# Root chains per group, placed behind GpSimd's output transfers, with the sums of y held back for VectorE's half sums

## The chip, the cores and the metric

The kernel runs on one core of one Trainium2 chip. The metric is the device time of one execution in microseconds (us). One profiled execution of the kernel before is at hand, and seven timed ones.

## The reference, cut to what matters

The input x has 8 sequences of 4224 rows with 192 channels. The first stage is a causal convolution along the rows with 7 taps, whose weights are a softmax per head (8 heads of 24 channels). Its result is called y here. The second stage normalises each row and adds a small network of two matrix products to it:

```python
w = softmax(weight)                                   # 8 heads x 7 taps
y = conv(x_padded, w)                                 # per head, 7 rows back
xn = (y - mean(y)) / sqrt(var(y) + 1e-6) * g_ln
out = y + maximum(xn @ w_ch1, 0) @ w_ch2              # 192 -> 768 -> 192
```

The kernel folds the mean and g_ln into w_ch1. The factor 1/sqrt(var + 1e-6) is positive, so it can be taken out of the relu and applied to the rows of the result at the very end. It is therefore not needed until a row's two products are done.

## The kernel before

**Groups.** The rows are cut into 18 groups (`groups`). Groups 0 to 2 are small (6, 8 and 10 columns of 128 rows). Groups 3 to 17 have 16 columns each, two groups per sequence. A loop over the groups does, for group g, an *up* stage (192 to 768, `up_mixed`) and a *down* stage (768 to 192, `down_fast`); the convolution of g + 1 and the first taps of g + 2 are woven in between. All instructions stand in the order in which the program writes them; each engine takes its own in that order, and semaphores make an engine wait for another one's results. So what stands ahead of an instruction on its engine holds it up.

**Products.** In groups 3 to 17 both stages are done with seven block products instead of eight, on the quarters of the operands. That needs sums of quarters. In the up stage these are sums of y: s3 and s2 (`sums_of_y`, L575 and L576, on GpSimd, called POOL in the profile), then s4 and the sum written over a21 (L578 and L579, on VectorE, DVE in the profile). TensorE (PE) takes first a11 and a12, which need no sum, then s2, s3, s1 (this is a21 with L579 in it), a22, s4, for one third of the hidden units, and then again in another order for the other two thirds. In the down stage PE does three products, then a fourth one, and meanwhile DVE does nine *half sums* in place (`half_sum`, L756, 128x1024 elements each): three for the fifth product, three for the sixth, three for the seventh. Three additions from PSUM (L820) follow on DVE.

**The row statistics.** `moments` lets DVE write six numbers per row (L439, 16 instructions). `root` makes 1/sqrt(var + 1e-6) of them on GpSimd, with 19 small instructions (L457 to L470) on a tile of one column per column of rows: two reads of the statistics, then a start value, and three Newton steps of four instructions each. Before the change one chain of `root` serves two groups, 3 with 4, 5 with 6, and so on: `chain_of` says which group's tile holds the statistics, and the call stands at the end of the loop's turn for odd g, after `down_fast(g)`, in which the moments of g + 1 are taken. Group 17 has a chain of its own.

**GpSimd's queue.** It also issues DMAs that add into their target. In one turn of the loop its instructions are, in order: three transfers in `up_mixed` that add a part of a product into the hidden tile (L583, room<-room), one more of each of two larger kinds (L583, parts_cs and parts_tb), two output transfers of the group before (L876, `add_to_out`), two transfers that add the second tap into y of g + 2 (L397, `second_tap`), the two sums of y of g + 1 (L575, L576), in odd turns `root`, and at the start of even turns a memset of padding rows (L160). The third of the L583 transfers must have landed before ScalarE (ACT) can overwrite what it read, and PE waits for that.

**ScalarE's list of work.** `up_mixed` returns a list (`work`) of ACT instructions that `down_fast` puts between the evictions of its first products: a relu, the scaling of the rows of the group before (with the two `add_to_out` behind the last of each half), two more relus; `down_fast` adds the first and second taps of g + 2 to it. Nine entries go behind the first product, six behind the second and six behind the third. With 17 entries ahead of the taps, both output transfers are issued by then; the second tap's transfers are the last entry, behind the later products. In the last group the list holds the three relus alone.

Of the kernel before, what the change touches and what calls it, by code (L numbers as in the profile page):

```python
# [16 lines left out]
def kernel(  # L17
# [29 lines left out]
    nc = tc.nc  # L47
# [377 lines left out]
    def chain_of(g):  # L425


        return g - g % 2 if g < 3 else g - 1 + g % 2

    def moments(g, j1=0, j2=None):  # L430
        n = groups[g][2]
        if j1:
            pass
        elif g == chain_of(g):
            sums[g] = spool.tile([P, 2 * J, nc.vector.BN_STATS_DIM], F32, tag="st", name=f"st{g}")
        else:
            sums[g] = sums[g - 1][:, groups[g - 1][2] :]
        for j in range(j1, n if j2 is None else j2):
            nc.vector.bn_stats(out=sums[g][:, j, :], in_=y[g][:, j, :])  # L439

    def root(g):
        both = [k for k in (g, g + 1) if k < NG and chain_of(k) == g]
        n = sum(groups[k][2] for k in both)
        st = sums[g]
        dt = spool.tile([P, 2 * J], F32, tag="d", name=f"d{g}")
        vt = spool.tile([P, 2 * J], F32, tag="v", name=f"v{g}")
        rt = spool.tile([P, 2 * J], F32, tag="r", name=f"r{g}")
        d, v, r = dt[:, 0:n], vt[:, 0:n], rt[:, 0:n]

        def affine(dst, src, scale, bias):  # L450
            nc.gpsimd.tensor_scalar(
                out=dst, in0=src, scalar1=scale, scalar2=bias, op0=ALU.mult, op1=ALU.add
            )

        nc.gpsimd.tensor_tensor(d, st[:, 0:n, 1], st[:, 0:n, 4], op=ALU.subtract)  # L457
        nc.gpsimd.tensor_tensor(v, st[:, 0:n, 2], st[:, 0:n, 5], op=ALU.add)
        nc.gpsimd.tensor_tensor(d, d, d, op=ALU.mult)
        affine(v, v, 1.0 / D, 1e-6)  # L460
        affine(d, d, 0.25, 0.0)
        nc.gpsimd.tensor_tensor(v, v, d, op=ALU.add)


        affine(r.bitcast(I32), v.bitcast(I32), -0.5, float(0x5F3759DF))
        for _ in range(3):
            nc.gpsimd.tensor_tensor(d, r, r, op=ALU.mult)  # L467
            nc.gpsimd.tensor_tensor(d, d, v, op=ALU.mult)
            affine(d, d, -0.5, 1.5)
            nc.gpsimd.tensor_tensor(r, r, d, op=ALU.mult)  # L470
        for k in both:
            rstd[k] = rt[:, (k - g) * groups[g][2] :]
# [95 lines left out]
    def sums_of_y(g, engine):  # L568

        room = upool.tile([P, 3 * HJ * CH * C], F32, tag="ys", name=f"ysums{g}")  # L570
        room = room.rearrange("p (v j c t) -> p v j c t", v=3, c=CH, t=width(g))
        s2, s3, s4 = [room[:, v] for v in range(3)]
        a11, a12, a21, a22 = quarters_of_y(g)
        ysums[g] = a21, s2, s3, s4
        engine.tensor_tensor(s3, a21, a11, op=ALU.subtract)  # L575
        engine.tensor_tensor(s2, s3, a22, op=ALU.add)  # L576
        yield
        nc.vector.tensor_tensor(s4, a12, s2, op=ALU.subtract)  # L578
        nc.vector.tensor_tensor(a21, a21, a22, op=ALU.add)  # L579
        yield  # L580
# [4 lines left out]
    def up_mixed(g, ahead):  # L585
# [103 lines left out]
        p.close(p.c22, Y, rooms[1][:, 0:PAIR])  # L689
        p.product(X, a22, p.t[2], False)  # L690
        p.relu(p.c11)
        lower_sum(g, (PAIR,))
        p.close(p.c21, X)
        p.product(Y, s4, p.b22, False)
# [7 lines left out]
        taps_of_next(5, 6, heads=(H // 2, H))  # L702
        taps_of_next(6, K)

        work = [lambda: one.relu(one.c22)]

        def scale_one(j):
            scale(g - 1, j, j + 1)
            if j == 7:
# [1 line left out]
            elif j == done - 1:  # L711
                add_to_out(g - 1, 8, done)

        if not last:
            work += [lambda j=j: scale_one(j) for j in range(2, done)]
        half = [lambda i=i: two.relu(two.c22[:, i : i + 1]) for i in range(PAIR)]
        return work[0:9] + half + work[9:]

# [53 lines left out]
    def down_fast(g, work):  # L772
        n = fast[g]
        t = width(g)
        w = n * T
        a = of_products(g)
        flat = cpool.tile([P, NC, NFAST * C], F32, tag="cs", name=f"cs{g}")[:, :, 0 : n * C]
        order = "p c (h j t) -> p c h j t" if t == C else "p c (j h t) -> p c h j t"
        cs = flat.rearrange(order, h=2, t=t)
        free = a[:, 1, 0].rearrange("p f q j t -> p (f q) j t")  # L780
        parts = [free[:, 0:CH], free[:, CH : 2 * CH]]
        banks = [take_bank() for c in range(CH) for i in range(2)]

        def product(bank, left, right, to, first, behind=0):
            for c in range(CH):
                dst = banks[2 * c + bank]
                for f in (PAIR, *range(PAIR)):
                    for q in range(NQ):
                        nc.tensor.matmul(  # L789
                            dst[C * q : C * q + C, 0:w], right[:, f, C * c : C * c + C],  # L790
                            left[:, f, q], start=(first and f == PAIR), stop=(f == PAIR - 1),
                            skip_group_check=True,
                        )
                if to is not None:
                    nc.scalar.copy(  # L795
                        to[:, c], dst[:, 0:w].rearrange("p (j t) -> p j t", t=t)
                    )
                for one in work[:behind]:
                    one()
                del work[:behind]  # L800

        b = quarters_of_w2()
        c11, c21 = cs[:, 0:CH, 0], cs[:, 0:CH, 1]
        c12, c22 = cs[:, CH:NC, 0], cs[:, CH:NC, 1]
        if g + 2 < NG:
            work += [
                lambda tap=tap, h=h: tap(g + 2, heads=(h, h + 1))
                for tap in (first_tap, second_tap) for h in range(H)
            ]
        product(0, a[:, 0, 0], b[0], c11, True, 3)  # L810
        product(1, a[:, 1, 0], w2sums[:, 2], c22, True, 2)
        product(1, a[:, 1, 1], w2sums[:, 3], c21, False, 2)
        product(1, a[:, 0, 1], b[2], None, True, 3)
        if g + 1 < NG:
            transpose(g + 1)
        half_sum(g, (1, 1), (1, 1), (1, 0), ALU.add)
        half_sum(g, (0, 0), (1, 1), (0, 0), ALU.add)
        half_sum(g, (0, 1), (0, 1), (1, 1), ALU.subtract)
        for c in range(CH):
            nc.vector.tensor_tensor(  # L820
                c11[:, c], c11[:, c], banks[2 * c + 1][:, 0:w].rearrange("p (j t) -> p j t", t=t),
                op=ALU.add,
            )
        product(0, a[:, 1, 1], w2sums[:, 1], parts[0], False, 2)
        product(0, a[:, 0, 0], w2sums[:, 0], parts[1], False, 2)
        for one in work:
            one()
        product(0, a[:, 0, 1], b[3], c12, False)
        if g + 1 < NG:
            moments(g + 1)  # L830
            sums = sums_of_y(g + 1, nc.gpsimd)
            next(sums)
            next(sums)
        else:
            finish_fast(g, 0, flat, cs, parts)
        return flat, cs, parts
# [105 lines left out]
    for g in range(NG):  # L942
        mixed, last = g in MIXED, g + 1 == NG
        if g + 2 < NG:
            load_x(g + 2)
        if mixed:
            work = up_mixed(g, ahead(g))
        else:
            up(g)
        if not fast[g]:  # L950

            conv(g + 1)
            transpose(g + 1)
            if g < 2:
                store_y(g + 1)
                moments(g)
            first_tap(g + 2)
            if g == 2:

                second_tap(g + 2)  # L960
                store_y(g + 1, nc.gpsimd)
            down(g)
            park(g)
            if g == 1:
                finish(0)
                root(0)
                sums_of_quarters([w2sums[:, v] for v in range(4)], *quarters_of_w2())
                moments(2)
                root(2)
                finish(1)  # L970
            elif g == 2:
                b11, b12, b21, b22 = quarters_of_w1()
                sums_of_quarters([b12] + [w1sums[:, v] for v in range(3)], b11, b12, b21, b22)
                later = sums_of_y(3, nc.vector)
                next(later)
                next(later)
                finish(2)
                moments(3)
            continue
        if g + 2 < NG:  # L980
            store_y(g + 1)
        results = down_fast(g, work)
        if last:
            finish_fast(g, 1, *results)
            add_and_store(g, slice(0, fast[g]))
            down(g)
            finish(g)
        else:
            if g % 2:
                root(g)  # L990
            if g + 2 == NG:
                root(g + 1)


# [28 lines left out]
```

## Time and profile before

| what | value |
|---|---|
| median of 7 timed runs | 985.5 us (983.26 to 987.48) |
| the profiled execution's own time | 985.5 us |
| its span in the trace | 983.8 us |
| granted TensorE clock, mean | 0.992 |
| TensorE matmul busy | 956.4 us, 97% |
| VectorE busy | 902.5 us, 92% |
| ScalarE busy | 680.8 us, 69% |
| GpSimd busy | 261.9 us, 27% |
| a down stage without a stall | 27.44 us |
| an up stage without a stall | 27.95 to 27.96 us |

The span is 1.7 us shorter than the time of the execution; that lies around it. A busy TensorE is not TensorE at its peak, but in this kernel the same 504 matmuls take the same time in every stage that has no stall, so that a longer stage tells of a wait. The rows of a timeline give the start in us, the time taken, the engine, the line, the operation and the tiles (written <- read); the brackets hold the idle time of the engine before it, and what ended it.

### The profile page before, as it was taken

The page shows a single profiled execution, that of the slowest core. Times are in us where ns is not written, and L with a number is a line of the kernel's source. Part 1 is how long each engine was busy: PE and PEld are TensorE (multiplying, and loading weights), DVE is VectorE, ACT ScalarE, POOL GpSimd, SP SyncE. Part 2 cuts the span into 40 slices and gives each one's busy share as a digit, 9 for nine tenths or more (in the row PEclk, how much of TensorE's full clock was granted, in tenths as well). Part 3 has the DMA queues.
Part 4 walks back from the last instruction along what each step waited for, and adds up shares of the span by engine and source line. Part 5 has one row for each costly group of instructions (what it writes and reads, how often), then busy time and mean ns, then how long its engine had stood idle before and what let it go on. Part 6 is the DMA issues. An engine that isn't in the chain of part 4 may idle for free.

```text
span 983.8 us, 38335 instructions
## 1 busy us (share of the span) xinstructions
PE 956.4 (97%) x17274; PEld 722.5 (73%) x17274; DVE 902.5 (92%) x1491; ACT 680.8 (69%) x1098; POOL 261.9 (27%) x383
## 2 busy tenths in 40 slices
PE   5999999999999999999999999999999999998997
PEld 5886586676968677685968678686867768695787
DVE  5899998979999899989999898989999899999757
ACT  4733769467786968777795868778695867775351
POOL 2004411612116131432117131432217121342200
PEclk8999999999999999999999999999999999999999
DMA  8343687579687796978787796968877796756031
GB/s 171 121 123 131 146 210 180 150 151 252 139 240 155 180 235 116 272 151 243 149 226 157 168 245 122 275 129 239 164 194 174 146 279 136 185 120 109 2 67 67
DMA packets 26386, 165.15 MB, mean 168 GB/s; under 512 B 3567, under 2 KB 4463, under 8 KB 18542
## 3 DMA queue, kind: packets, MB, share of 16 engines
q0 software_dynamic: 19120, 99.36, 51.7%
q1 hardware_dynamic: 6798, 63.34, 17.4%
q8 instruction: 135, 2.21, 0.9%
q14 instruction: 29, 0.24, 0.1%
q10 hardware_dynamic: 304, 0.00, 0.0%
HBM read 38.95 MB, written 50.33 MB: 91 GB/s over the span
## 4 chain that ended last, share of the span: by engine, by line
PE 77%; DVE 8%; DMA 7%; POOL 4%; ACT 2%; issue 1%; SPq 0%; ACTq 0%; DVEq 0%; POOLq 0%
PE ps L521 37%; PE ps L789 34%; PE ps L736 6%; DVE room L756 6%; DMA room<-room 5%; DVE st L439 2%; DMA xg<-in_x_dram 1%; ACT room L616 1%; POOL d L457 1%; PE ps L320 1%; POOL d L467 1%; POOL room L583 1%; DMA ga<-in_moe_g_ln_dram 1%; POOL r L470 1%; DVE room L622 0%
## 5 line engine op out<-in xcount | busy, mean ns | idle before, releaser
L408 DVE SCALAR_TENSOR_TENSOR y<-xg,taps,y 128x384 f32<-128x384 f32 (+3 forms) x734 | 367.2, 578 | 2.4 <-ACT y L383 2.0
L789 PE MATMUL ps<-room,w2sums 128*32 128x256 f32 (+1 forms) x4320 | 237.4, 377 | 4.1 <-DVE room L756 3.1
L521 PE MATMUL ps<-yt,w 32*128 32x256 f32 (+2 forms) x4104 | 238.6, 379 | 0.0
L616 ACT COPY room<-ps 128x1024 f32<-128x1024 f32 (+1 forms) x132 | 172.0, 1303 | 85.8 <-PE ps L521 78.6
L521 PEld LDWEIGHTS ps<-yt,w 32*128 32x128 f32 x4104 | 203.6, 185 | 27.5 <-issue 7.0
L789 PEld LDWEIGHTS ps<-room,w2sums 128*32 128x32 f32 x4320 | 140.5, 110 | 96.2 <-DVE room L756 6.7
L789 PE MATMUL ps<-room,w 128*32 128x256 f32 (+1 forms) x3240 | 180.3, 375 | 2.5 <-DVE room L756 2.4
L756 DVE TENSOR_TENSOR room<-room 128x1024 f32<-128x1024 f32 (+1 forms) x135 | 157.8, 1242 | 7.6 <-PE ps L789 7.6
L789 PEld LDWEIGHTS ps<-room,w 128*32 128x32 f32 x3240 | 105.1, 110 | 70.4 <-DVE room L622 5.2
L521 PE MATMUL ps<-ysums,w1sums 32*128 32x256 f32 x2160 | 124.1, 377 | 0.0
L521 PEld LDWEIGHTS ps<-ysums,w1sums 32*128 32x128 f32 x2160 | 110.7, 185 | 9.6 <-issue 2.7
L795 ACT COPY cs<-ps 128x256 f32<-128x256 f32 (+1 forms) x180 | 66.4, 372 | 45.6 <-PE ps L789 45.6
L629 ACT ACTIVATE room<-room 128x1024 f32<-128x1024 f32 (+1 forms) x75 | 90.8, 1236 | 10.2 <-DMA room<-parts_cs 9.9
L869 ACT ACTIVATE ot<-ot,r 128x192 f32<-128x192 f32 x232 | 93.8, 463 | 0.0
L876 POOL DMA_DIRECT2D out_dram<-ot x40 | 34.4, 1084 | 206.0 <-ACT ot L869 127.8
L622 DVE TENSOR_TENSOR room<-room,ps 128x2048 f32<-128x2048 f32 (+1 forms) x20 | 42.5, 2128 | 47.0 <-PE ps L521 46.8
L383 ACT ACTIVATE y<-xg,taps 128x384 f32<-128x384 f32 (+3 forms) x141 | 72.8, 611 | 9.6 <-DMA out_dram<-y 6.9
L521 PE MATMUL ps<-yt,w1sums 32*128 32x256 f32 x1080 | 66.6, 386 | 5.3 <-ACT room L616 5.3
L439 DVE BATCH_NORM_STATS2 st<-y 128x6 f32<-128x192 f32 x264 | 70.2, 342 | 0.0
L795 ACT COPY room<-ps 128x256 f32<-128x256 f32 (+1 forms) x90 | 33.8, 375 | 48.5 <-PE ps L789 44.5
L521 PE MATMUL ps<-ysums,w 32*128 32x256 f32 x1080 | 64.8, 378 | 0.0
L521 PEld LDWEIGHTS ps<-yt,w1sums 32*128 32x128 f32 x1080 | 54.7, 189 | 12.8 <-ACT room L616 9.8
(103 smaller groups left out, 905.9 us busy)
## 6 DMA issues: line engine op xcount, KB each, us to landing
xg<-in_x_dram SPq DMA_DIRECT2D x15, 2112.0 KB, 17.6
out_dram<-ot POOLq DMA_DIRECT2D x29, 768.0 KB, 8.8
y<-tb POOLq DMA_DIRECT2D x28, 768.0 KB, 10.7
room<-room POOLq DMA_DIRECT2D x42, 512.0 KB, 5.9
out_dram<-y SPq DMA_DIRECT2D x13, 1536.0 KB, 10.1
room<-parts_cs POOLq DMA_DIRECT2D x14, 1024.0 KB, 8.9
room<-parts_tb POOLq DMA_DIRECT2D x14, 1024.0 KB, 7.5
xg<-in_x_dram SPq DMA_DIRECT2D x1, 1536.0 KB, 7.5
```

The lines of the kernel that those rows point to most:

```text
L383: nc.scalar.mul(y[g][:, 0:n, cs], xg[g][:, 0:n, cs], taps[:, h, 0:1])
L408: nc.vector.scalar_tensor_tensor(out=y[g][:, 0:n, cs], in0=t[:, k : k + n, cs], scalar=taps[:, h, k : k + 1], in1=y[g][:, 0:n, cs], op0=AL ...
L439: nc.vector.bn_stats(out=sums[g][:, j, :], in_=y[g][:, j, :])
L521: nc.tensor.matmul(banks[:, q, i * w : i * w + w], right[rows, c, P * i : P * i + P], left[rows, :, c, :], start=(first and c == 0 and i = ...
L616: nc.scalar.activation(dst, src, AF.Relu) if relu else nc.scalar.copy(dst, src)
L622: nc.vector.tensor_tensor(c, c, self.seen(banks), op=ALU.add)
L629: nc.scalar.activation(c, c, AF.Relu)
L736: nc.tensor.matmul(bank[C * q : C * q + C, 0:w], w2[:, f, C * c : C * c + C], left, start=(f == 0), stop=(f == NF - 1),)
L756: nc.vector.tensor_tensor(a[:, *dst, f], a[:, *left, f], a[:, *right, f], op=op)
L789: nc.tensor.matmul(dst[C * q : C * q + C, 0:w], right[:, f, C * c : C * c + C], left[:, f, q], start=(first and f == PAIR), stop=(f == PAI ...
L795: nc.scalar.copy(to[:, c], dst[:, 0:w].rearrange("p (j t) -> p j t", t=t))
L869: nc.scalar.mul(ots[g][:, j, :], ots[g][:, j, :], rstd[g][:, j : j + 1])
```

## The change

There are five edits.

1. `chain_of`: only groups 0 and 1 share a chain; each later group has its own, with tiles of 16 columns instead of 32.
2. `root(g)` is called in `down_fast(g)`, after the third product. On GpSimd it stands behind both output transfers (L876) and ahead of the second tap's transfers (L397) and of the sums of y of g + 1 (L575, L576). The calls at the end of the loop's turn go.
3. In `sums_of_y` on GpSimd, DVE first sets one element of s3 to zero. GpSimd's first sum overwrites it and so waits for DVE to come to that memset, which stands behind the half sums and the three additions.
4. The order in the program becomes: memset, the two GpSimd sums, the moments of g + 1 on DVE, and the two DVE sums. In each engine's own order only the memset is new.
5. In the last group the relus of the two parts of c22 are done in `up_mixed`, ahead of `lower_sum`, the second part as one instruction instead of two; the list of work is empty.

```diff
     def chain_of(g):
-        return g - g % 2 if g < 3 else g - 1 + g % 2
+        return 0 if g < 2 else g
...
-            sums[g] = spool.tile([P, 2 * J, nc.vector.BN_STATS_DIM], F32, tag="st", name=f"st{g}")
+            sums[g] = spool.tile([P, J, nc.vector.BN_STATS_DIM], F32, tag="st", name=f"st{g}")
...
-        dt = spool.tile([P, 2 * J], F32, tag="d", name=f"d{g}")
+        dt = spool.tile([P, J], F32, tag="d", name=f"d{g}")
...
         ysums[g] = a21, s2, s3, s4
+        if engine is not nc.vector:
+            nc.vector.memset(s3[:, 0:1, 0:1, 0:1], 0.0)
         engine.tensor_tensor(s3, a21, a11, op=ALU.subtract)
...
         p.relu(p.c11)
+        if last:
+            one.relu(one.c22)
+            p.relu(p.c22)
         lower_sum(g, (PAIR,))
...
-        work = [lambda: one.relu(one.c22)]
-        if not last:
-            work += [lambda j=j: scale_one(j) for j in range(2, done)]
+        if last:
+            return []
+        work = [lambda: one.relu(one.c22)]
+        work += [lambda j=j: scale_one(j) for j in range(2, done)]
...
         product(1, a[:, 1, 1], w2sums[:, 3], c21, False, 2)
+        root(g)
         product(1, a[:, 0, 1], b[2], None, True, 3)
...
         if g + 1 < NG:
-            moments(g + 1)
             sums = sums_of_y(g + 1, nc.gpsimd)
             next(sums)
+            moments(g + 1)
             next(sums)
...
-        else:
-            if g % 2:
-                root(g)
-            if g + 2 == NG:
-                root(g + 1)
```

## The prediction on record

> **What bounds the kernel now.** The page's first part comes first: TensorE is busy for 956.4 of 983.8 us. I then cut the trace at PE's stage boundaries and looked at those stretches one by one, since 504 equal matmuls take 27.95 us in an up stage and 27.44 us in a down stage when nothing waits. The table by stretches has the stretch, its length, then busy us (and instructions) of PE, PEld, DVE, ACT and POOL, the granted clock and DMA:
>
> ```profile
> 154.94:184.97 30.03, 27.64 (x508) 16.52 (x505) 30.00 (x40) 20.85 (x45) 8.04 (x6) 1.00 0.87 232
> 184.97:216.82 31.85, 29.93 (x508) 26.55 (x504) 26.43 (x44) 20.27 (x17) 13.76 (x25) 0.95 0.55 110
> 411.33:439.29 27.96, 27.96 (x508) 25.36 (x504) 25.63 (x41) 20.02 (x17) 13.52 (x25) 1.00 0.75 151
> 522.38:551.35 28.97, 28.25 (x509) 25.26 (x505) 25.48 (x42) 20.27 (x17) 13.77 (x25) 1.00 0.72 146
> 579.09:607.04 27.95, 27.95 (x507) 25.35 (x504) 25.27 (x40) 19.88 (x17) 4.33 (x5) 1.00 0.74 148
> 887.60:919.90 32.30, 29.20 (x509) 16.06 (x505) 32.11 (x45) 15.17 (x36) 8.09 (x5) 0.95 0.41 71
> ```
>
> The reader should see that most stages are already at their floor, and that the excess sits in few: the down stages of groups 3 (first row) and 16 (last), and up stages of even groups, where POOL has 25 instructions instead of 5. That is the root chain. The chain of waits around up(10) says how it reaches PE:
>
> ```profile
> 522.49 2.66 POOL d L457
> ...
> 533.46 1.16 POOL room L583 x2
> 534.62 9.32 DMA room<-room
> ...
> 544.04 1.88 ACT room L616
> ```
>
> L583 stands behind root on POOL. It is issued about 8 us later than in an odd group, lands at 543.94, and ACT, then PE, wait. The two down stages have another cause, seen in the timeline of group 16:
>
> ```profile
> 899.80 13.51 DVE L756 TENSOR_TENSOR room<-room 128x1024 f32<-128x1024 f32 x9
> 900.03 2.65 POOL L575 TENSOR_TENSOR ysums<-yt 128x768 f32<-128x768 f32 x1
> 902.76 2.66 POOL L576 TENSOR_TENSOR ysums<-ysums,yt 128x768 f32<-128x768 f32 x1
> 906.55 9.53 PE L789 MATMUL ps<-room,w2sums 128*32 128x256 f32 x144 [3.10 <-DVE room L756]
> ```
>
> POOL's sums run beside the half sums. These take 13.51 us instead of 10.27 in undisturbed groups, POOL's second sum 2.66 instead of 1.84: they block each other, and PE waits 3.10 us.
>
> **What it removes.** (a) Root leaves the place ahead of L583. Excess of the up stages that root lengthens, from the lengths: up(4) 31.85 - 27.96 = 3.89, up(10) 28.97 - 27.96 = 1.01, up(12) 1.47 and up(14) 1.44 by the same subtraction, up(6) 0.62 (0.86 less 0.24 at another step), up(8) and up(16) nothing. Sum 8.43. (b) The memset makes the sums wait behind the half sums: down(3) 30.03 - 27.44 = 2.59 and down(16) 32.30 - 27.44 = 4.86, sum 7.45. In the other groups the wait is empty, as the sums come after the second tap's transfers anyway (517.08, half sums over at 517.25). (c) In the last group ACT does the three relus between two evictions:
>
> ```profile
> 951.68 2.96 ACT L629 ACTIVATE room<-room 128x1024 f32<-128x1024 f32 x3
> 954.53 1.13 ACT L795 COPY cs<-ps 128x176 f32<-128x176 f32 x5
> ```
>
> The second product takes 3.81 us there, its neighbours 2.79 and 2.71: 1.1 us. The new place is ACT's idle 4.26 us ahead of 948.64, which takes all 2.96. Together 8.43 + 7.45 + 1.10 = 17.0 us.
>
> **What it adds.** The memset: L216, also a memset of one column, took 0.06 us. It costs nothing where DVE has to wait behind the moments anyhow (below); otherwise 0.1 x 14 = 1.4 us at most. Seven more chains on POOL cost only what they delay. Behind root on POOL wait the two L397 transfers, L575, L576, the padding memset and L583; for L576 waits DVE's L578, and for both PE's third product. So the question is when root ends. I take group 9 as the model (down stage from 494.94, up(10) from 522.38).
>
> Root can start when the second L876, issued at 506.80, lets it: 0.57 later, as L575 follows L876 in group 16 (899.46 to 900.03). That is 507.37. The nine half sums run from 506.99 to 517.25. So root now lies beside them. What does a small POOL instruction do beside DVE work with two inputs in SBUF? Root(2) ran beside the taps (L408, a start every 0.53 us):
>
> ```profile
> 90.21 0.46 POOL L468 TENSOR_TENSOR d<-d,v 128x10 f32<-128x10 f32 x1
> 90.75 0.44 POOL L451 TENSOR_SCALAR d<-d 128x10 f32<-128x10 f32 x1
> 91.28 0.45 POOL L470 TENSOR_TENSOR r<-r,d 128x10 f32<-128x10 f32 x1
> ```
>
> Their cadence is 0.53 us too, against 0.30 when DVE does transposes or moments: one POOL instruction per DVE instruction, each done when one of DVE's ends. DVE itself isn't slowed (L578 takes 0.94 us in odd and even groups). Root's first instruction does worse. It reads statistics 24 bytes apart:
>
> ```profile
> 918.55 1.74 POOL L457 TENSOR_TENSOR d<-st 128x16 f32<-128x16 f32 x1 [13.14 <-DVE st L439]
> ```
>
> It ends with the second of two DVE instructions, and in the paired chains (2.66 us) with the third of three; unblocked it took 0.24.
>
> The half sums come every 1.14 us, so nine of them let nine of root's 19 instructions through, eight if L457 takes two. I take eight, by the 16-column row, which is nearest. Eleven are left at 517.33 and take 11 x 0.298 = 3.3 us: root ends near **520.6**. Before, POOL was free until ACT released L397 at 515.97:
>
> ```profile
> 515.97 1.76 POOL L397 DMA_DIRECT2D y<-tb  x2 [8.30 <-ACT room L795]
> 517.08 2.51 POOL L575 TENSOR_TENSOR ysums<-yt 128x768 f32<-128x768 f32 x1
> 519.68 1.84 POOL L576 TENSOR_TENSOR ysums<-ysums,yt 128x768 f32<-128x768 f32 x1
> ```
>
> From L397 to the end of L576 it is 5.54 us (515.97 to 521.51), so s2 is there at 526.2 instead of 521.5. PE wants it at 525.18 and stalls 1.0 us. DVE waits longer: it is through with the moments at 522.4 and starts L578 at 526.2, 3.88 us later than the 522.33 of before. What slack has DVE? In an up stage without a stall its one idle time is ahead of L622:
>
> ```profile
> 492.56 2.29 DVE L622 TENSOR_TENSOR room<-room,ps 128x2048 f32<-128x2048 f32 x1 [2.15 <-PE ps L521]
> ```
>
> PE's next down stage waits for the end of L622 (494.85, PE at 494.94), and from there to the half sums DVE has 12.1 us of work without a gap, PE's three products 11.8. So DVE can lose 2.15 us per group, and what exceeds it lengthens the period: 3.88 - 2.15 = 1.73 us, PE's 1.0 included. This holds in the groups with second tap, half sums and root together: 4 to 15, twelve. 12 x 1.73 = **20.8 us**.
>
> Two groups escape. In group 3 root starts about 162, mostly beside transposes, and ends before ACT releases L397 at 173.35. In group 16 there is no L397: root ends about 913.4, the sums at 917.3, and PE, with up(17) moved forward to 915.04, wants s2 at 917.8.
>
> Of the later L397 transfers: they land 10.7 us after issue in the median, so about 532; the taps that need them start behind the delayed DVE at 533.6. At the longest landing, 14.4 us, 2 us per group would come on top; I take nothing. L583 is issued about 527.3 instead of 533.5, close to the 526.6 that an odd group has, so (a) stays gained. In the last group root stands behind L876 at 941.34, ends by 950, and is wanted at 970.33: nothing.
>
> **Sum.** 20.8 - 17.0 = +3.8 us. The profiled execution took 985.5 us, 1.7 more than its span and equal to the median of the seven, so the forecast is 985.5 + 3.8 = **989.3 us**.
>
> The unknown is how many of root's instructions are left when the half sums end; each moves the sum by 0.298 x 12 = 3.6 us. Ten: 985.7. Eight: 978.5. Fourteen, if the second reader of the statistics (L458) and L457 take three each as the 32-column rows have it: 1000. On SBUF — State Buffer, section Who interferes with whom, the Trainium skill says that a VectorE instruction with two SBUF inputs and a GpSimd instruction that reads SBUF exclude each other, and that whoever comes second waits for the whole other instruction. That speaks against putting root beside the half sums; by it L457 would wait for one instruction, not two, which gives ten left and 985.7. The rows of L457 say at least two, and I follow them.
>
> **Rivals.**
> 1. *Root slips through* (the other side: faster). If two independent instructions pass at one end of a half sum (L457, L458 and L459 are issued 0.19 apart when free), or if small readers aren't held by this form of DVE instruction, root ends earlier. The deciding point is 520.3 for the end of root: before it the sum is negative, and from 518.5 on downwards all of the 17.0 us stay: 968.5. For it: no row shows root beside half sums. Against: L467 waited all 0.98 us of a plain TENSOR_TENSOR (L842) at 526.90. Times 968.5 to 983.
> 2. *Root starves.* In all eight contended rows L457 ended only when DVE's run of two-input instructions was over. If that is the rule for strided reads, root begins at 517.33, ends at 522.8, and L578 starts at 528.3: 6.0 - 2.15 = 3.85, x 12 = 46 us, in all 1015. PE's stall would then be 3.1 us, and in group 16 such a stall was followed by 144 matmuls in 9.36 us instead of 7.77, clock 0.57: up to 1 us more per group, 1027. TensorE: Matmul & The Clock Gate, section What's actually happening, puts the clock gate's idle window at about 3.4 us; by it 3.1 us would often pass unpunished and 1015 would stand. Against this rival: unstrided instructions get in at every DVE end.
> 3. *It evens out.* Ten left, or DVE's slack a little larger: within 2 us of before.
>
> **Chances.** A measurement here can tell some 0.2%, 2 us, from no change. Forecast case (10.5 to 14 left; 987.5 to 1000): 0.40. Rival 1: 0.33. Rival 2: 0.12. Rival 3: 0.15. Slower 0.52, within 0.15, faster 0.33. As cases of both signs carry much of it, the range runs from 967 (rival 1 whole, and 1.5 for the memset's order and the clock) to 1004 (14 left and some of the late landings), and leaves out rival 2; the forecast case alone has 987.5 to 1000.
>
> **What would show it.** Right: up(4) near 28, down(3) and down(16) near 27.5 us; L583 about 4 to 5 us into every up stage; root's first eight instructions 1.1 us apart beside L756 and the rest 0.3; L397 near 25.7 us into the down stage instead of 21.0; DVE idle some 3.8 us ahead of L578 and none ahead of L622; down and up together near 57.1 us instead of 55.4. Wrong: L397 still at 21.0 and DVE never waiting for L576 (rival 1), or L457 taking 8 us or more (rival 2), or half sums above 1.22 us each, which I have excluded.

## The result and the profile after

The changed kernel takes **989.13 us** (median of 13 runs, 988.65 to 991.04); the kernel before took 984.97 us beside it (median of 34 runs). The ratio is 1.0048, 95% interval 1.0039 to 1.0057: slower by 0.5%, and 0.2 us from the forecast of 989.3. The span of the profiled execution is 988.5 us, 4.7 us more than before.

The table by stretches answers to the first one of the prediction (stretch, its length, then busy us and instructions of PE, PEld, DVE, ACT and POOL, granted clock, DMA). The stretches are down(3), up(4), up(10), up(15), down(16) and the products of the last down stage:

```profile
154.69:182.13 27.44, 27.44 (x508) 16.12 (x504) 27.40 (x44) 20.85 (x45) 17.13 (x26) 1.00 0.87 241
182.13:210.09 27.96, 27.96 (x508) 25.35 (x505) 25.59 (x41) 20.28 (x17) 5.17 (x6) 1.00 0.64 125
...
523.20:552.79 29.59, 28.11 (x509) 25.24 (x505) 25.64 (x41) 20.60 (x18) 8.81 (x9) 1.00 0.79 155
...
808.50:840.67 32.17, 29.53 (x508) 26.32 (x504) 25.74 (x41) 20.27 (x17) 9.41 (x9) 0.95 0.74 145
897.73:925.21 27.48, 27.48 (x505) 16.18 (x505) 27.40 (x44) 14.84 (x35) 15.41 (x23) 1.00 0.47 82
954.56:973.47 18.91, 18.91 (x505) 16.30 (x509) 12.35 (x19) 7.80 (x21) 0.00 (x0) 1.00 0.06 12
```

The two long down stages and up(4) are at their floor now, and the last stage has lost 1.1 us. In exchange the up stages 5 to 11, 14 and 16, odd and even alike, have 29.58 to 29.60 us instead of a floor of 27.96, and up(15) has 32.17. The cause stands in GpSimd's timeline of the stage that the prediction took as its model, group 9 (its down stage now starts at 495.72, up(10) at 523.20):

```profile
507.82 1.27 POOL L457 TENSOR_TENSOR d<-st 128x16 f32<-128x16 f32 x1
...
517.22 1.08 POOL L468 TENSOR_TENSOR d<-d,v 128x16 f32<-128x16 f32 x1
518.39 0.20 POOL L451 TENSOR_SCALAR d<-d 128x16 f32<-128x16 f32 x1
...
521.57 1.80 POOL L397 DMA_DIRECT2D y<-tb  x2 [0.29 <-issue]
...
525.30 1.81 POOL L579 TENSOR_TENSOR ysums<-ysums,yt 128x768 f32<-128x768 f32 x1
...
528.04 0.60 POOL L586 DMA_DIRECT2D room<-room  x1
```

(The same statement has another line number in another kernel. Here L578 and L579 are GpSimd's sums that were L575 and L576, and L581 is VectorE's sum that was L578; L586 was L583, L762 was L756, L625 was L622, TensorE's L795 was L789 and ScalarE's L801 and L619 were L795 and L616.) From 507.82 to 518.30 root gets one instruction through per half sum, nine beside nine; so it is in all groups from 4 to 16. Only then do the other ten follow, 0.3 us apart, and behind them the second tap's transfers and the sums, which end at 527.11. L586 is issued 4.84 us into up(10); before it was 11.08 us. In VectorE's and TensorE's timelines of the same group, in stretches, one sees who pays:

```profile
507.82 9.25 DVE L762 TENSOR_TENSOR room<-room 128x1024 f32<-128x1024 f32 x8
...
516.99 1.23 DVE L762 TENSOR_TENSOR room<-room 128x1024 f32<-128x1024 f32 x1
...
527.14 0.96 DVE L581 TENSOR_TENSOR ysums<-yt,ysums 128x768 f32<-128x768 f32 x1 [3.75 <-POOL ysums L579]
...
550.45 2.28 DVE L625 TENSOR_TENSOR room<-room,ps 128x2048 f32<-128x2048 f32 x1
```

```profile
527.16 2.87 PE L521 MATMUL ps<-ysums,w1sums 32*128 32x256 f32 x48 [1.09 <-ACT room L619]
...
552.79 3.44 PE L795 MATMUL ps<-room,w 128*32 128x256 f32 x60 [0.39 <-DVE room L625]
```

VectorE waits 3.75 us for GpSimd's sum. The 2.15 us of idle time that it had ahead of L625 are used up (no bracket on that line), so TensorE begins the next down stage late. The 1.09 us ahead of TensorE's product on s2 are put down to ScalarE's L619, but that product starts 0.05 us after L579 ends; in the list of waits the same place has "PEld ps L521 <- POOL ysums L579", 17.9 us in 12 waits.

### The profile page after: what moved, and what is told of

It reads as the page before. It is cut to its first block, busy times and chain, and to the rows that moved or that the text cites. A ratio compares the mean times of both kernels' runs of the same rounds, so it can differ in the third digit from the quotient of the medians.

```text
span 988.5 us, 38488 instructions
## 1 busy us (share of the span) xinstructions
PE 954.6 (97%) x17274; PEld 720.7 (73%) x17274; DVE 897.2 (91%) x1505; ACT 681.9 (69%) x1097; POOL 361.1 (37%) x516
## 5 line engine op out<-in xcount | busy, mean ns | idle before, releaser
L521 PE MATMUL ps<-yt,w 32*128 32x256 f32 (+2 forms) x4104 | 238.4, 379 | 0.0
L619 ACT COPY room<-ps 128x1024 f32<-128x1024 f32 (+1 forms) x132 | 172.0, 1303 | 94.5 <-PE ps L521 94.5
L795 PE MATMUL ps<-room,w2sums 128*32 128x256 f32 (+1 forms) x4320 | 235.4, 375 | 0.3 <-DVE room L762 0.3
L521 PEld LDWEIGHTS ps<-yt,w 32*128 32x128 f32 x4104 | 203.6, 185 | 27.6 <-issue 7.0
L795 PEld LDWEIGHTS ps<-room,w2sums 128*32 128x32 f32 x4320 | 140.8, 110 | 90.0 <-DVE room L762 4.9
L795 PE MATMUL ps<-room,w 128*32 128x256 f32 (+1 forms) x3240 | 181.9, 375 | 4.9 <-DVE room L625 4.3
L795 PEld LDWEIGHTS ps<-room,w 128*32 128x32 f32 x3240 | 105.4, 110 | 74.3 <-DVE room L625 10.3
L762 DVE TENSOR_TENSOR room<-room 128x1024 f32<-128x1024 f32 (+1 forms) x135 | 152.9, 1201 | 6.4 <-PE ps L795 6.4
L521 PE MATMUL ps<-ysums,w1sums 32*128 32x256 f32 x2160 | 125.4, 381 | 13.6 <-ACT room L619 9.8
L521 PEld LDWEIGHTS ps<-ysums,w1sums 32*128 32x128 f32 x2160 | 110.2, 187 | 25.9 <-POOL ysums L579 17.9
L801 ACT COPY cs<-ps 128x256 f32<-128x256 f32 (+1 forms) x180 | 65.7, 366 | 44.4 <-PE ps L795 44.3
L876 ACT ACTIVATE ot<-ot,r 128x192 f32<-128x192 f32 x232 | 93.4, 458 | 0.0
L801 ACT COPY room<-ps 128x256 f32<-128x256 f32 (+1 forms) x90 | 33.4, 371 | 48.2 <-PE ps L795 47.8
L586 POOL DMA_DIRECT2D room<-room x42 | 35.2, 839 | 85.1 <-ACT room L619 83.8
L521 PE MATMUL ps<-ysums,w 32*128 32x256 f32 x1080 | 64.8, 378 | 0.0
L521 PE MATMUL ps<-yt,w1sums 32*128 32x256 f32 x1080 | 64.5, 377 | 0.0
L394 ACT ACTIVATE tb<-xg,taps 128x384 f32<-128x384 f32 x112 | 61.7, 630 | 0.0
```

The costliest lines, as they stand in the source:

```text
L394: nc.scalar.mul(tb[g][:, 0:n, cs], xg[g][:, 1 : 1 + n, cs], taps[:, h, 1:2])
L521: nc.tensor.matmul(banks[:, q, i * w : i * w + w], right[rows, c, P * i : P * i + P], left[rows, :, c, :], start=(first and c == 0 and i = ...
L586: nc.gpsimd.dma_start(out=dst, in_=src, accum_op=ALU.add)
L619: nc.scalar.activation(dst, src, AF.Relu) if relu else nc.scalar.copy(dst, src)
L762: nc.vector.tensor_tensor(a[:, *dst, f], a[:, *left, f], a[:, *right, f], op=op)
L795: nc.tensor.matmul(dst[C * q : C * q + C, 0:w], right[:, f, C * c : C * c + C], left[:, f, q], start=(first and f == PAIR), stop=(f == PAI ...
```

## Where the 4.7 us come from

Stage lengths of after, less those of before. Two rows are excess over the 27.96 us of an up stage without a stall: the first is that of before, the fifth that of after. In the even stages only their difference was measured.

| term | predicted | measured |
|---|---|---|
| root no longer ahead of L586: the old excess of up(4) to up(14) | -8.43 | -8.67 |
| sums no longer beside the half sums: down(3) | -2.59 | -2.59 |
| the same: down(16) | -4.86 | -4.83 |
| relus of the last group | -1.10 | -1.15 |
| root holds up the sums: up(5) to up(16) | +20.8 | +20.61 |
| the other down stages | 0 | +1.02 |
| up(17) | 0 | +0.56 |
| ahead of group 3 | 0 | -0.25 |
| sum | +3.8 | +4.7 |

## The experiments

The theory is the prediction's: root's place beside the half sums lets one of its instructions through per half sum; what is left delays the sums of y by more than VectorE's slack. Its rivals: the new wait (the memset) itself costs the time; the other order of edit 4 does; or a chain for each group is too much for GpSimd wherever it stands.

**The wait alone.** Before, with edits 3 and 4 only; two groups share a chain, which stands where it stood.

```diff
+        if engine is not nc.vector:
+            nc.vector.memset(s3[:, 0:1, 0:1, 0:1], 0.0)
...
-            moments(g + 1)
             sums = sums_of_y(g + 1, nc.gpsimd)
             next(sums)
+            moments(g + 1)
```

> The kernel before with the memset and the order of the sums (edits 3 and 4) and nothing else; root stays in its old place, one chain for two groups. My theory: the wait is empty in most groups, frees the half sums of groups 3 and 16 (down(3) 30.03 to 27.44 us, down(16) 32.30 to 27.44), and lets up(4) come down from 3.89 us over its floor to about 1, as DVE is no longer late there. Sum 7.5 to 10.5 us less than before, 974 to 978. Rival 'the wait for VectorE is what makes the changed kernel slower': slower than before here, by the 21 us that the twelve up stages lost.

976.03 us, ratio 0.992 (0.9903 to 0.9936). Down(3), up(4) and down(16), by stretches:

```profile
154.29:181.73 27.44, 27.44 (x508) 16.14 (x504) 27.40 (x45) 20.85 (x45) 7.17 (x6) 1.00 0.87 240
181.73:210.97 29.24, 28.25 (x509) 25.27 (x505) 25.50 (x41) 20.27 (x17) 13.75 (x25) 1.00 0.60 120
884.66:912.10 27.44, 27.44 (x509) 16.16 (x505) 27.41 (x45) 15.04 (x35) 5.41 (x4) 1.00 0.47 84
```

The wait costs nothing and wins the two down stages whole: the rival that it is the cause falls. Up(4) says something that the prediction had wrong. It falls from 31.85 to 29.24 us though root stands where it stood. TensorE's wait in it falls from 1.92 to 0.99 us, as VectorE is no longer late after the collision in down(3). The other 1.7 us are the clock (0.95 over the stage then, 1.00 now). Only 1.3 of the 3.89 us of excess, in this execution, belonged to root's place.

**The relus alone.** Before, with edit 5 only.

```diff
         p.relu(p.c11)
+        if last:
+            one.relu(one.c22)
+            p.relu(p.c22)
...
+        if last:
+            return []
```

> The kernel before with the last group's lower right relus moved forward and nothing else. If the tail term is right, only the last down stage changes: 20.05 us becomes 18.9, the wait of its first product on ScalarE (0.94 us) goes, all other stages keep their lengths, and the time falls by 1.1 us (ratio 0.999). Rival: the moved relus delay ScalarE's own work in the last up stage; then that stage grows from 28.80 us by what the tail wins, and the time stays.

983.77 us, ratio 0.9985 (0.9973 to 0.9998), or -1.4 us. The products of the last down stage:

```profile
943.93:962.83 18.90, 18.90 (x505) 16.31 (x508) 12.35 (x19) 7.77 (x21) 0.00 (x0) 1.00 0.06 12
```

The last stage loses 1.15 us and up(17) keeps its 28.80: ScalarE did have room there, and the rival falls. This trace, taken in an execution of 979.59 us, holds a warning too. Edit 5 touches no group but the last, yet up(4) has 30.16 us in it (31.85 before), up(6) 28.05 (28.82), up(12) 28.72 (29.43): the excess of the even stages differs between executions by up to 1.7 us. In up(4) these 1.7 us are the clock alone: down(3) is as long as before and TensorE waits the same 1.92 us, but behind that wait the clock fell before and stays at 1.00 here. So of the 3.89 us of up(4) 0.9 belonged to the collision and 1.7 to a drop of the clock that need not come. The 8.43 us of term (a) were read from one execution; in this one the same stages have 5.6.

**After without the wait.** The memset is taken out, and the sums may start beside the half sums where root lets them.

```diff
-        if engine is not nc.vector:
-            nc.vector.memset(s3[:, 0:1, 0:1, 0:1], 0.0)
```

> The changed kernel without the memset; root stays beside the half sums. My theory: only group 3 feels it, where the sums come right behind the second tap's transfers and meet the half sums again: down(3) 30 us instead of 27.44, and 0 to 1 us in up(4), so 989 + 2.6 to 3.6 = about 992. Group 16 stays at 27.5, as there root alone keeps the sums back behind the half sums. Up stages of groups 5 to 16 stay at 29.6. Rival 'the wait is the cost': up stages back at 28.0, 970 or less.

992.13 us, ratio 1.0091 (1.0074 to 1.0107). Down(3), by stretches:

```profile
154.79:187.13 32.34, 29.33 (x508) 17.41 (x504) 32.31 (x44) 20.84 (x45) 18.87 (x26) 0.95 0.80 217
```

Down(3) was expected at 30 us: TensorE waits 3.01 us in it, 2.39 before, and here the clock drops behind that. The 992 us were met even so; up(15) is 1.06 us shorter than in the changed kernel (31.11 us, without a drop of the clock). Most of the other up stages that root lengthens have 29.56 us or close to it. So the memset has no part in the loss, and in the changed kernel it earns 4.9 us in down(3) alone. Down(16) has 27.47 us without it too: root, now ahead of the sums, holds them back by itself until 926.89, past the half sums. The prediction gave that stage's gain to the memset; either edit alone brings it.

**One Newton step more, one less.** A change of four instructions per chain tells what the rest of root costs behind the half sums. The first number of `range` in the two kernels is 4 and 2 instead of 3.

```diff
-        for _ in range(3):
+        for _ in range(4):
```

> The changed kernel with four Newton steps in root instead of three: 23 instructions instead of 19 on GpSimd. My theory: the four come behind the half sums, 0.298 us each, and move the end of root, the sums and L581 by 1.19 us; DVE has no slack left, so each of twelve up stages goes from 29.6 to 30.8 us: +14.3, about 1003. Where PE's stall at s2 grows from 1.09 to 2.3 us the clock may drop, which cost 1.6 us a time in other places: up to 1022. Rival 'root isn't on the path; later transfers or their competition are the cost': within 3 us of 989.

> The changed kernel with two Newton steps instead of three: the last refinement of 1/sqrt is left out, 15 instructions instead of 19. My theory: L397, the sums and L581 come 1.19 us earlier, each of twelve up stages goes from 29.6 to 28.4 us: -14.3, and up(15), whose 2.6 us stall was followed by a lower clock, gives 1 to 1.5 more: 973 to 975. Rival 'the work of root doesn't matter, only that its 10 us of blocked time lie there': same as the changed kernel, 989, as nine instructions are held by the nine half sums anyway.

Four steps: 1009.68 us, ratio 1.0267 (1.0245 to 1.0289). Two steps: 974.45 us, ratio 0.99 (0.9877 to 0.9923). Most up stages have 30.73 to 30.77, 29.58 and 28.38 to 28.41 us with four, three and two steps: 1.17 to 1.18 us for four instructions, which at 0.298 each are 1.19. What root has left behind the half sums goes into the period in full, once VectorE's slack is gone. With four steps something comes on top. Here are up(8) and up(16) of that kernel (up(15) has 34.43 us and a clock of 0.90):

```profile
411.16:442.96 31.80, 29.56 (x509) 26.68 (x505) 25.73 (x42) 20.16 (x17) 9.94 (x10) 0.95 0.74 146
...
883.90:914.66 30.76, 28.10 (x508) 25.24 (x504) 25.64 (x41) 20.48 (x18) 9.26 (x9) 1.00 0.77 152
```

In up(8) and up(16) TensorE waits 2.24 and 2.27 us ahead of the product on s2, which is nearly the same. After the one the clock falls and the stage is 1 us longer; after the other it stays at 1.00. Stretches of 3.41 us around the two waits, of up(8) and then of up(16), show the difference:

```profile
414.10:417.51 3.41, 1.23 (x24) 1.18 (x28) 1.25 (x2) 1.01 (x1) 3.33 (x4) 1.00 1.11 225
417.51:420.92 3.41, 3.41 (x40) 2.93 (x36) 3.38 (x6) 1.19 (x2) 0.25 (x1) 0.50 0.97 192
420.92:424.33 3.41, 3.41 (x68) 2.97 (x64) 3.31 (x6) 2.63 (x3) 0.82 (x1) 1.00 0.44 82
...
885.14:888.55 3.41, 1.63 (x32) 1.17 (x24) 0.00 (x0) 2.02 (x2) 3.33 (x3) 1.00 1.01 201
888.55:891.96 3.41, 2.92 (x52) 2.58 (x56) 2.91 (x4) 1.01 (x1) 1.25 (x2) 1.00 1.01 202
```

The clock is at 0.50 for 3.41 us, and at 1.00 on both sides. The next two drops of this kernel begin at 475.53 and 769.08, which is 17 and 103 times 3.413 us after 417.51: they lie on a grid. The stretches of the grid are those shown. In up(8) nearly the whole wait lies in one of them, in which TensorE idles 2.18 us; in up(16) a line of the grid cuts it into 1.78 and 0.49 us. TensorE: Matmul & The Clock Gate, section What's actually happening, in the Trainium skill, has an idle window of about 3.4 us that runs freely, whatever the program does. That stalls of one length are punished at one time and not at another agrees with a free-running window, and so does the length of the drop. A window need not be idle from end to end: 2.18 us of its 3.41 were enough, and here the measurement decides.

**Root elsewhere: right behind the up stage.** The call goes from `down_fast` to the loop, behind `up_mixed`. On GpSimd it then stands behind the last L586 and ahead of the output transfers.

```diff
         product(1, a[:, 1, 1], w2sums[:, 3], c21, False, 2)
-        root(g)
...
             work = up_mixed(g, ahead(g))
+            root(g)
```

> The changed kernel with root(g) called right behind the up stage of g: on GpSimd behind the last transfer of parts_tb (L586) and ahead of the output transfers, where GpSimd idles 8 us; VectorE then does L625, L771 and taps, not half sums. Chains per group, memset and moved relus stay. My theory: place is all; L397 goes out when ACT releases it (21.0 us into the down stage), VectorE doesn't wait for s2, all of the 17 us of gains stay: about 968. The first output transfer is issued 1 to 2 us later and nobody waits for it. Rival 'seventeen chains instead of ten cost wherever they stand': 985 or more.

**966.11 us**, ratio 0.9821 (0.9803 to 0.9838), span 963.9 us, clock 1.000. Up(11) by stretches, and GpSimd's timeline around root(11), down(11) starting at 596.51:

```profile
568.55:596.51 27.96, 27.96 (x508) 25.35 (x504) 25.63 (x41) 20.26 (x17) 5.90 (x13) 1.00 0.80 159
```

```profile
594.19 0.57 POOL L457 TENSOR_TENSOR d<-st 128x16 f32<-128x16 f32 x1
...
596.64 1.20 POOL L468 TENSOR_TENSOR d<-d,v 128x16 f32<-128x16 f32 x1
...
617.53 1.76 POOL L397 DMA_DIRECT2D y<-tb  x2 [8.29 <-ACT room L801]
620.05 1.83 POOL L578 TENSOR_TENSOR ysums<-yt 128x768 f32<-128x768 f32 x1 [0.76 <-DVE ysums L577]
```

All up stages from 4 to 16 but one (28.11) have 27.96 us. The same 19 instructions lie beside an addition from PSUM, two instructions of 1.2 us (L468 is held by one of them) and taps of 0.53 us; root ends at 603.76, 13.8 us ahead of L397, and L397 goes when ScalarE releases it, 21.0 us into the down stage as before. The rival that a chain per group is too much for GpSimd falls, and so does that of edit 4's order, which stands in this kernel. This version beats both the kernel before and the changed one.

**The same without the wait.**

```diff
-        if engine is not nc.vector:
-            nc.vector.memset(s3[:, 0:1, 0:1, 0:1], 0.0)
```

> Root behind the up stage, as in the fastest version so far, without the memset. My theory: the memset is worth something only where the sums reach GpSimd ahead of the half sums' end: down(3) back to 30 to 32.4 us, down(16) back to 32.3: 7.4 to 9.8 us more than with it, 973.5 to 976. Rival 'with root out of the way the wait is needless': 966.

974.85 us, ratio 0.9909 (0.989 to 0.9929). Down(3) has 30.02 and down(16) 31.92 us, nearly what they had before; the other stages are as with the wait, within 0.3 us. With root out of the way the memset earns both stages' excess.

**Root elsewhere: behind the sums.** The call stands behind the two sums on GpSimd, so that nothing of root is ahead of them.

```diff
-        root(g)
...
             next(sums)
+            root(g)
             moments(g + 1)
```

> The changed kernel with root(g) on GpSimd behind the two sums of y of g + 1, so in its old place, but for each group and without waiting for moments, since those of g are a stage old. My theory: L397 and the sums are on time, DVE waits for nothing; root starts at 522 in the model's time, is held by three DVE instructions, ends near 530, and L586 follows at 530 to 532, later than the 526.6 of an undisturbed group and earlier than the 533.5 of before. Up stages of both parities 0 to 0.5 us over their floor: 966 to 972. Rival 'any root ahead of L586 costs PE what it cost before': 8.4 us for even groups and as much again for odd ones, 983.

972.72 us, ratio 0.9888 (0.9868 to 0.9907). The loss beside the half sums is gone, and root stands ahead of L586 again, now in every group. GpSimd's timeline at the start of up(8), from 405.71:

```profile
405.53 0.24 POOL L457 TENSOR_TENSOR d<-st 128x16 f32<-128x16 f32 x1
405.73 2.80 POOL L458 TENSOR_TENSOR v<-st 128x16 f32<-128x16 f32 x1
...
416.32 2.40 POOL L586 DMA_DIRECT2D room<-room  x3
```

L586 is issued 10.6 us into the stage, later than the 7.6 to 9.6 us expected; up stages vary from 27.95 to 29.11 us, some more than 0.5 us over their floor, and the time lies just above the expected range. This is the old trouble of the even groups, in a smaller size.

**Half sums cut in two.** If one instruction passes per half sum, twice as many half sums of half the size let twice as many through.

```diff
-                a[:, *dst, f], a[:, *left, f], a[:, *right, f], op=op
+                a[:, *dst, f, q], a[:, *left, f, q], a[:, *right, f, q], op=op
```

(`q` runs over the two halves of the columns, inside the loop over `f`.)

> The changed kernel with each half sum as two instructions of 128x512 instead of one of 128x1024; root untouched. If GpSimd gets one instruction in at each end of a DVE instruction, eighteen of root's nineteen go through beside the half sums instead of nine, at 0.6 us each, and root ends near 519 instead of 521.3 in the model's time. DVE pays some 0.7 us more for the half sums, 0.2 of it ahead of PE's fifth product. DVE's wait for s2 falls from 3.75 us to about 1; up stages near 28.0 to 28.6, down stages near 27.7: 972 to 982. Rival 'GpSimd is held by the work of the half sums, however it is cut' (the port's share, or starved until they end): root ends as late or later, and the half sums take longer: 989 to 998.

973.09 us, ratio 0.9886 (0.9868 to 0.9903). Root in group 9 of that kernel:

```profile
504.82 0.54 POOL L462 TENSOR_TENSOR v<-v,d 128x16 f32<-128x16 f32 x1
...
513.02 1.80 POOL L397 DMA_DIRECT2D y<-tb  x2 [0.29 <-issue]
```

The cadence, the time from one start to the next, falls from 1.15 to 0.61 us, which is that of the halves. Seventeen instructions pass beside eighteen halves, as L457 ends only with the second; two are left at the end instead of ten, VectorE's wait for the sums is 1.37 us, below its slack, and the up stages (up(15) apart, 29.29) are at 27.96 us. The price is in the down stages: VectorE's half sums take 11.20 us in all, and most of these stages 27.70 instead of 27.44.

## Why the prediction was right, step by step

The time, the mechanism of the loss and the stages that lose and gain by it were as forecast. Several terms of the sum were not, and their errors cancelled. In us from the start of down(9), which strips off the shift of the stages ahead of it:

| step of the prediction | predicted | measured |
|---|---|---|
| root starts | 12.43 | 12.10 |
| root's instructions through beside nine half sums | 8 | 9 |
| half sums end | 22.31 (as before) | 22.50 |
| root's instructions left | 11 | 10 |
| L397 is issued | 25.66 | 25.85 |
| the sum L579 ends | 31.26 | 31.39 |
| TensorE's stall ahead of s2 | 1.0 | 1.09 |
| VectorE's wait ahead of L581 | 3.8 | 3.75 |
| down and up together | 57.1 | 57.07 |

*The sum as written.* From its own terms the sums end at 526.14 (520.6 + 5.54), not 526.2, and the loss is 12 x 1.66 = 19.9 us, not 20.8, which makes the time 988.4; the end of root from which nothing is lost is 518.9, not 518.5.

*One instruction per half sum* held exactly, in the groups from 4 to 16. It had been carried over from taps of 0.53 us to half sums of 1.14 us without a row of that pair.

*L457 takes two* was wrong: in the model group it ends with the first half sum (1.27 us). So ten are left, and by the prediction's own alternative that gave 985.7 us. This is the rule of the Trainium skill, SBUF — State Buffer, section Who interferes with whom, by which the one that comes second waits for one whole instruction of the other; in this kernel it agrees with the row. In the kernel with root behind the sums it does not: there L458 takes 2.80 us beside three instructions of VectorE, as L457 did in the paired chains, and beside the halved half sums L457 ends with the second. What makes a read of the statistics wait for three in one place and one in another was not found.

*What made up for the eleventh instruction.* In the model group it is two things. The first of the ten starts 22.67 us into the stage instead of 22.39. And there is an idle time of 0.29 us between root and L397 ("issue"), where the prediction ran the two together; it stands in eleven of the twelve groups from 4 to 15, where root's last instruction took 0.22 us (group 14 has more, see below), and not in group 3, where that instruction was held for 1.07 us beside a half sum. Half sums beside root take 10.40 us in nine instead of 10.27; the first three have up to 1.26 us, above the 1.22 that the prediction excluded, but the sum of that is 0.13 us.

Outside the model group it is three terms that were taken as nothing. Up(15) is 2.6 us longer than its neighbours: L397 starts 1.65 us behind root there instead of 0.29, TensorE stalls 2.64 us, and behind that the clock is at 0.50 for 3.4 us (0.95 over the stage). Without the memset the same stage had a stall of 2.61 us, no drop and 31.11 us, so about 1.1 of the 2.6 us are the clock. The profile puts the late L397 to ScalarE, but much the same 1.36 us stand ahead of this transfer in all eleven kernels, wherever root ended: in the kernel before its idle time was 9.66 us there and 8.28 to 8.31 in the other groups from 4 on, which VectorE's slack hid. Up(17) loses 0.56 us: the prediction asked only when TensorE wants s2 there, but VectorE waits 1.64 us for the sums too, and its first L625 starts 3.57 us into the stage instead of 3.01. The down stages lose 1.02 us net (1.2 in groups 11 and 12, where the up stages lose less: up(12) and up(13) have 28.77 and 28.91 us); down(11) has 28.31 us with the relus alone too, so this need not be the change.

*Group 3* escaped, though not as forecast. Root's last six instructions lay beside half sums, and L397 went out at 173.70, 19.0 us into the stage (18.4 before). Nobody lost by it, as the sums wait for the memset until 178.27.

*The gains* came out within 0.25 us each. For up(4) that hides a wrong reason: only 1.3 of its 3.89 us belonged to root's place, 0.9 to the collision in down(3) and 1.7 to the clock. All three are gone in the changed kernel, so the sum did not show it. For down(16), root's own place would have been enough.

*The rivals.* That root slips through is refuted: never do two instructions pass at one half sum in groups 4 to 16. That root starves is refuted as well: L457 does not wait for the end of the run. That it evens out was nearest to what happened to the count of instructions, and the small terms above moved the time back to the forecast. A hit within 0.2 us thus has an error of 3.6 us in one term and others of the same size against it.

*Still open*: the waits for two and three instructions, and the 1.36 us ahead of L397 in group 14.

## What to carry to other kernels

In these runs a chain of small GpSimd instructions beside VectorE instructions with two inputs in SBUF went forward by one instruction per VectorE instruction (a start every 1.15, 0.61 or 0.53 us), however short its own were; only reads of the statistics took longer in places. So it is cheap beside short ones, or beside transposes and moments (0.30 us), and dear beside long ones, and the question of where to put it is which of VectorE's stretches lies there and who stands behind it in GpSimd's queue. Here the same 19 instructions in another place are worth 23 us (966.1 against 989.1). A wait that costs nothing by itself can earn much when it keeps two engines from working on long operands at the same time: the memset of one column is worth 8.7 us (974.85 against 966.11). The time is lost only beyond the slack of the engine that waits: here 2.15 us of VectorE's, and past that 1.2 us per four instructions in each of twelve groups.

## What the runs showed of the hardware

- Nine half sums beside nine of root's instructions cost VectorE 0.13 us in all, while each of GpSimd's took 1.05 to 1.27 us instead of 0.20 to 0.24. Two long streams are another case: half sums beside a 128x768 sum make both slower (13.51 instead of 10.27 us in group 16 before).
- Halving the size of VectorE's instructions halves the cadence of GpSimd's beside them (1.15 to 0.61 us); the halves cost VectorE 0.93 us more per nine (11.20 us against 10.27).
- A drop of TensorE's clock lasts 3.41 us at 0.50 (6.83 us behind a stall of 3.80 us), and what brings it is not the length of a stall alone but how much of it falls into one stretch of a fixed grid of 3.413 us. From group 3 on, in the profiles of all eleven kernels, each of the nine stretches with 2.17 us or more of idle time was followed by a drop, and none with 1.78 us or less. In between lie three: 1.92 us with a drop in the kernel before, 1.92 and 1.94 us without one with the relus alone. The four stalls of 2.97 to 3.10 us in these runs were all followed by a drop.
